# Cached attention on one core: K of a pack by two transfers instead of four, wide V by one instead of two

## The chip, the cores and the metric

The kernel runs on one core of a Trainium2 chip. The metric is the device time of one execution, in microseconds (us). A core has five engines that each work through a program of their own: PE (matrix products), ACT, DVE and POOL (elementwise work), and SP, which here does nothing but issue DMA transfers. Transfers run on 16 DMA engines, each of which takes packets from queues; one queue (q1) holds what SP issues, another (q10) what ACT issues. Engines wait for each other, and for transfers, by semaphores.

## The reference

Two independent attention blocks, A and B, of the same shape; their outputs stand side by side.

```python
B, Sq, D = 16, 64, 640            # batch, queries, model width
H, Sk, Dh = 32, 512, 128          # heads, cached keys, head width; all bfloat16
q = (x @ wq).reshape(B, Sq, H, Dh).transpose(0, 2, 1, 3)
scores = einsum("bhqd,bhkd->bhqk", q, k_cache) * Dh ** -0.5
o = einsum("bhqk,bhkd->bhqd", softmax(scores), v_cache)
out = o.transpose(0, 2, 1, 3).reshape(B, Sq, H * Dh) @ wo
# result: concatenate([out_A, out_B], axis=-1)
```

Each of the four caches (K and V of A and of B) has 16 × 32 × 512 × 128 values, 67.1 MB; every value is read once.

## The kernel before

**Tiling.** The work is cut into 128 packs. A pack is 4 heads of 2 batches (a batch pair), so 1 MB of K and 1 MB of V. Four packs with j = 0 to 3 cover 16 heads of one pair; eight pairs make a phase; four phases (two halves of the heads, two blocks) make the whole. The weights WQ and WO of the next phase are loaded while a phase ends.

**A pack's steps**, by the names in the code, with the lines of the profile: QP (L607, PE) projects the queries, KT (L621, DVE, two halves) transposes K in 32×32 blocks, S (L631, PE) forms the scores, EX (L650, ACT) takes the exponentials and row sums, RC (L663, DVE) and NM (L679, POOL) normalise, TR (L690, PE) and TE (L700, DVE) transpose the probabilities, PV (L714, PE) multiplies with V, OE (L722, ACT) copies out, OP (L734, PE) multiplies with WO and adds up.

**Loads.** LDK (L556) brings K of a pack into one of six buffers of `kn_ring`. It is four transfers of 256 KB: for each batch b and each half l, 32 rows of 8 KB go to the partitions 2b + l, 2b + l + 4, and so on. LDV (L567, L569) brings V into one of four buffers of `v_ring`, one transfer of 512 KB for each batch. Packs with j in `WIDE = (0, 1, 2)` have rows of 4 KB, one for each of 128 partitions (L567); the fourth has two rows of 2 KB in each partition (L569). LDX, LDWQ and LDWO bring x and the weights; some of these are issued by ACT.

**Order.** `build_plan` lists every operation with a due time in packs (`AT`) and sorts each engine's list by it; SP's list is sorted by the time from which a load may start. A V load may be issued once PV of the pack four before is done. K loads stand behind V loads in SP's list and have no wait of their own that lasts. From reads and writes the plan derives what each operation waits for. All transfers of a pack's K count on one semaphore, and so do those of its V. Because transfers of one semaphore may finish in any order, `wait_count` rounds a wait up to a whole pack by the table `PARTS`: four parts for K, two for V. KT therefore waits for all four K transfers, and PV for both V transfers:

```python
PARTS = dict(d_v=2, d_k=4)
...
def wait_count(d):
    part = PARTS.get(d.sem[0], 1)
    return -(-d.count // part) * part
```

A second program for very large or small sums stands behind the first and is not run here.

Of the kernel before, what the change touches and what calls it, by code (L numbers as in the profile page):

```python
# [14 lines left out]
SUM_MAX = 2.0 ** 40  # L15


PARTS = dict(d_v=2, d_k=4)


class Cfg:
    NK = 6
    NV = 4
# [36 lines left out]
def build_plan(dims, cfg, general):  # L60
# [12 lines left out]
    def add(eng, kind, idx, ts, reads=(), writes=()):  # L73
        op = Op(eng, kind, idx, ts, reads, writes)
        ops.append(op)
        at[(kind, idx)] = op
        return op

    def add_output(n):
        g, j = n // NJ, n % NJ  # L80
        final = n >= 0 and dims["FINAL"](g // NBP)
        for b in range(2):
            tv = n + AT["PV"]
            op = add("sp", "LDV", (n, b), tv - 0.3, [], [("v" if n >= 0 else "absent", n % cfg.NV, b)])
            loads.append((n - cfg.NV + AT["PV"] + 0.2 if n >= 0 else -99.0, 3, op))
        if n > -2:
            add("pe", "TR", n, n + AT["TR"], [("pn", i) for i in range(4)] + [("ident",)], [("B", 4), ("B", 5)])
        for b in range(2):
            add("dve", "TE", (n, b), n + AT["TE"][b], [], [("B", 4 + b), ("pT", b)])
        add("pe", "PV", n, n + AT["PV"], [("pT", 0), ("pT", 1), ("v", n % cfg.NV, 0), ("v", n % cfg.NV, 1)],  # L90
            [("B", 4), ("B", 5), ("B67",)])
        add("act", "OE", (n, 1), n + AT["OE"][0], [], [("B67",), ("oT", 1)])
        add("act", "OE", (n, 0), n + AT["OE"][1], [], [("B", 4), ("B", 5), ("oT", 0)])
        add("act", "ZO", n, n + AT["ZO"], [("zeros",)], [("B67",)])
        add("pe", "OP", n, n + AT["OP"], [("oT", 0), ("oT", 1), ("wo", j)], [("B67",)])
        if j == NJ - 1:
            bp = g % NBP
            add("dve", "OS", g, n + AT["OS"], [("acc", bp)], [("B67",), ("out_sb",) if final else ("acc", bp)])
            if final:
                add("act", "ST", g, n + AT["ST"], [("out_sb",)], [("out_dram", g)])  # L100
# [17 lines left out]
    for ph in range(NPH):  # L118
        twp = [ph * PH + j + (AT["WP1"] if ph else AT["WP0"]) for j in range(NJ)]
        for kt in range(dims["KT"] if ph else 0):  # L120
            ready = twp[-1] - PH + 0.5 if ph > 1 else NJ - 1 + AT["WP0"] + 0.5
            op = add("sp", "LDWQ", (ph, kt), twp[0] - 0.5, [], [("ws", kt, j) for j in range(NJ)])
# [17 lines left out]
    for n in range(-2, N):  # L140
        add_output(n)
        if n < 0:
            continue
        g, j = n // NJ, n % NJ
        add("pe", "QP", n, n + AT["QP"], [("xT", g % cfg.NX), ("wqp", j)], [("SB", 1)])
        add("act", "QE", n, n + AT["QE"], [], [("SB", 1), ("qs", n % cfg.NQ)])
        for i in range(4):
            op = add("sp", "LDK", (n, i), n + AT["KT"][0] - 0.9, [], [("kn", n % cfg.NK)])
            loads.append((n - cfg.NV + AT["PV"] + 0.2 - cfg.KLEAD, 2, op))
        for b in range(2):  # L150
            tk = n + AT["KT"][b]
            add("dve", "KT", (n, b), tk, [("kn", n % cfg.NK)], [("kt", n % cfg.NKT, b)])
        add("pe", "S", n, n + AT["S"], [("qs", n % cfg.NQ), ("kt", n % cfg.NKT, 0), ("kt", n % cfg.NKT, 1)],
            [("SB", i) for i in range(4)])
        for i in range(4):
            h = 4 * n + i
            te = n + AT["EX"][i]
            if general:
                add("dve", "MX", h, te - 0.002, [], [("SB", i), ("negmax", h % 4)])
            add("act", "EX", h, te, [("negmax", h % 4)] if general else [],  # L160
                [("SB", i), ("p", h % cfg.NP), ("rs", h)])
            add("pool" if n < N - 1 else "dve", "NM", h, n + (AT["NM"] if n < N - 1 else AT["NMZ"])[i], [("p", h % cfg.NP), ("recip", n % cfg.NR, i // 3)], [("pn", i)])
        for a in range(2):
            add("dve", "RC", (n, a), n + AT["RC"][a], [("rs", 4 * n + i) for i in ((0, 1, 2), (3,))[a]],
                [("recip", n % cfg.NR, a)])
# [158 lines left out]
class Clocks:  # L324
# [15 lines left out]
    def finish(self, eng, op):  # L340
        ck = self.clock[eng]
        self.val[op.sem] = self.val.get(op.sem, 0) + 1
        c2 = dict(ck)
        if op.dma:
            c2[op.sem] = op.count
        else:
            self.own[eng][op.sem] = op.count
            for s2, v2 in self.own[eng].items():
                if c2.get(s2, 0) < v2:
                    c2[s2] = v2  # L350
        part = PARTS.get(op.sem[0], 1)
        for k in range(op.count - 1, (op.count - 1) // part * part, -1):
            for s2, v2 in self.snap[(op.sem, k)].items():
                if c2.get(s2, 0) < v2:
                    c2[s2] = v2
        self.snap[(op.sem, op.count)] = c2


def wait_count(d):
    part = PARTS.get(d.sem[0], 1)  # L360
    return -(-d.count // part) * part


def order_waits(progs, need, base):
    ks = Clocks(base)

    def visit(eng, op):
        want = {}
        for d in need[id(op)]:
            want[d.sem] = max(want.get(d.sem, 0), wait_count(d))  # L370
        if any(ks.val.get(s, 0) < v for s, v in want.items()):
            return False
        ck = ks.clock[eng]
        cand = [(s_, v_) for s_, v_ in want.items() if ck.get(s_, 0) < v_]
        keep = list(cand)
        for w in list(cand):
            for o in keep:
                if o != w and ks.snap[o].get(w[0], 0) >= w[1]:
                    keep.remove(w)
                    break  # L380
        op.waits = keep
        ks.learn(eng, keep)
        ks.finish(eng, op)
        return True

    run_order(progs, visit)
# [46 lines left out]
def mha_kernel(nc, blocks, out, cfg=None):  # L433
    cfg = cfg or Cfg()
# [16 lines left out]
    for general in (False, True):  # L451
        dims = dict(NPH=NPH, NBP=NBP, NJ=NJ, KT=KT, FIRST=lambda ph: ph % NSUB == 0,
                    FINAL=lambda ph: ph % NSUB == NSUB - 1)
        plans.append(build_plan(dims, cfg, general))
    NK, NV, NKT, NX, NXN, NQ, NP, NR = (cfg.NK, cfg.NV, cfg.NKT, cfg.NX, cfg.NXN, cfg.NQ, cfg.NP, cfg.NR)

    with contextlib.ExitStack() as es:
        block = es.enter_context(nc.Block())

        def sb(name, shape, dt):  # L460
            return es.enter_context(nc.sbuf_tensor(name, shape, dt))
# [4 lines left out]
        kn_ring = sb("kn_ring", [128, NK, 2, 2048], BF16)  # L466
        kt_ring = sb("kt_ring", [128, NKT, 32, 2, 2, 16, 2], BF16)
        v_ring = sb("v_ring", [128, NV, 2, 16, DH], BF16)
# [31 lines left out]
        def pack_info(n):  # L500
            g, j = n // NJ, n % NJ
            ph = g // NBP
            return ph // NSUB, g % NBP, j, ph % NSUB * HPH + 4 * j
# [46 lines left out]
            return ins, ins  # L550

        def em_LDK(e, op):
            n, b, l = op.idx[0], op.idx[1] // 2, op.idx[1] % 2
            blk, bp, j, h = pack_info(n)
            src = blocks[blk][1][2 * bp + b, h:h + 4].rearrange("h (p l t) d -> l (h p) (t d)", l=2, t=32)[l]
            ins = e.dma_start(kn_ring[2 * b + l::4, n % NK].rearrange("p a c -> p (a c)"), src)  # L556
            return ins, ins

        def em_LDV(e, op):
            n, b = op.idx  # L560
            if n < 0:
                return None, None
            blk, bp, j, h = pack_info(n)
            src = blocks[blk][2][2 * bp + b, h:h + 4]
            dst = v_ring[:, n % NV, b]
            if j in WIDE:
                ins = e.dma_start(dst.rearrange("p t d -> p (t d)"), src.rearrange("h (p t) d -> (h p) (t d)", t=16))  # L567
            else:
                ins = e.dma_start(dst.rearrange("p (a t) d -> p a (t d)", a=2),  # L569
                                  src.rearrange("(a s) (p t) d -> (s p) a (t d)", s=2, t=8))  # L570
            return ins, ins
# [340 lines left out]
```

## Time and profile before

| what | value |
|---|---|
| runs, us | 747.2, 747.67, 748.57; median 747.67 |
| profiled execution, us from first to last instruction | 747.1 |
| busy: PE, DVE, ACT, POOL | 91%, 69%, 70%, 54% of the span |
| moved by DMA | 295.15 MB, mean 395 GB/s |
| queue of SP (q1) / of ACT (q10), share of 16 engines | 94.1% / 5.0% |
| granted TensorE clock | 0.985 |
| transfers of K / of V | 512 of 256 KB / 256 of 512 KB |
| V, issue to landing, median | 12.4 us (A), 13.3 us (B) |

The profile is of one execution; it gives no other time of that execution than its span, which is 0.57 us below the median of the timed runs. A busy share is an average over stages, so the prediction reads each stage by itself. "SPq" is SP's issuing of transfers; it lasts longer when the queue that it feeds is full. The packet records list every DMA packet with queue, start, duration and size, but not the engine that carried it.

### The profile page before, as it was taken

What the parts mean: (1) busy time and instruction counts of PE and PEld (TensorE: products, weight loads), DVE (VectorE), ACT (ScalarE), POOL (GpSimd) and SP (SyncE); (2) the same over time, 40 slices, a digit from 0 to 9 for tenths busy, and PEclk for the clock granted to TensorE, in tenths of its full rate; (3) what the DMA queues carried; (4) which work ended last, traced back from release to release, by engine and by line L of the source; (5) the groups of instructions that cost most, each with busy time, mean ns of one, the idle gap of its engine ahead of it and who ended that gap; (6) DMA issues with size and microseconds to landing.
All of it is one profiled execution on the core that took longest, in us unless ns stands there. A gap on an engine that the chain in (4) does not pass through costs nothing.

```text
span 747.1 us, 57746 instructions
## 1 busy us (share of the span) xinstructions
PE 681.3 (91%) x26518; PEld 530.5 (71%) x26518; DVE 514.9 (69%) x818; ACT 519.7 (70%) x1559; POOL 404.0 (54%) x580
## 2 busy tenths in 40 slices
PE   2779999999999999999988999999997999999994
PEld 2557777777777777777766777777775777777773
DVE  6437777777777677676755676677676677877773
ACT  1438787787777677766756777777775677777772
POOL 3635555655965545545674455455486555555550
PEclk9879999999999999999999999999999999999998
DMA  9999999999999999999999999999999999999970
GB/s 326 391 402 411 412 411 414 411 410 413 405 400 415 411 414 411 412 413 414 410 400 406 410 413 413 412 410 410 413 407 402 410 413 413 413 414 411 410 301 17
DMA packets 87518, 295.15 MB, mean 395 GB/s; under 512 B 13360, under 2 KB 28208, under 8 KB 71088
## 3 DMA queue, kind: packets, MB, share of 16 engines
q1 hardware_dynamic: 76064, 281.43, 94.1%
q10 hardware_dynamic: 11408, 13.27, 5.0%
q14 instruction: 37, 0.30, 0.1%
q8 instruction: 9, 0.15, 0.1%
HBM read 292.03 MB, written 2.62 MB: 394 GB/s over the span
## 4 chain that ended last, share of the span: by engine, by line
SPq 35%; PE 30%; DMA 19%; POOL 5%; issue 4%; ACT 3%; DVE 3%; ACTq 0%; DVEq 0%
SPq L556 23%; PE ps L714 8%; DMA kn_ring<-in_A_k_cache_dram 8%; PE ps L734 7%; PE ps L607 6%; SPq L567 6%; DMA v_ring<-in_B_v_cache_dram 5%; SPq L569 5%; PE ps L631 4%; DMA kn_ring<-in_B_k_cache_dram 4%; PE ps L690 4%; POOL pn_sb L679 4%; DMA ws_sb<-in_A_wq_dram 2%; ACT p_ring L650 2%; ACT oT_sb L722 1%
## 5 line engine op out<-in xcount | busy, mean ns | idle before, releaser
L679 POOL TENSOR_SCALAR pn_sb<-p_ring,recip 128x512 bf16<-128x512 bf16 x508 | 341.8, 692 | 305.5 <-DVE recip L663 305.4
L621 DVE STREAM_TRANSPOSE kt_ring<-kn_ring 128x1024 f32<-128x1024 f32 x256 | 313.5, 1230 | 146.1 <-DMA kn_ring<-in_B_k_cache_dram 103.9
L650 ACT ACTIVATE p_ring<-ps 128x512 bf16<-128x512 f32 x512 | 298.9, 598 | 28.7 <-DMA xn_ring<-in_B_x_dram 6.7
L700 DVE COPY pT_sb<-ps 128x1024 bf16<-128x1024 bf16 x258 | 163.6, 674 | 71.6 <-PE ps L690 68.5
L714 PE MATMUL ps<-pT_sb,v_ring 32*128 32x64 bf16 (+1 forms) x14528 | 163.8, 192 | 26.1 <-DMA v_ring<-in_B_v_cache_dram 11.7
L714 PEld LDWEIGHTS ps<-pT_sb,v_ring 32*128 32x128 bf16 (+1 forms) x14528 | 146.6, 92 | 43.0 <-DMA v_ring<-in_B_v_cache_dram 14.5
L607 PE MATMUL ps<-xT_ring,wqp_sb 128*128 128x128 bf16 x2560 | 166.6, 221 | 7.6 <-POOL xT_ring L596 7.3
L734 PE MATMUL ps<-wo_sb,oT_sb 128*128 128x320 bf16 x1040 | 166.6, 303 | 3.3 <-issue 2.3
L607 PEld LDWEIGHTS ps<-xT_ring,wqp_sb 128*128 128x128 bf16 x2560 | 158.0, 114 | 14.7 <-issue 7.5
L722 ACT ACTIVATE oT_sb<-ps 128x256 bf16<-128x256 f32 x260 | 85.6, 381 | 116.7 <-PE ps L714 116.7
L631 PE MATMUL ps<-kt_ring,qs_ring 32*64 32x512 bf16 x4096 | 139.5, 384 | 0.0
L690 PEld LDWEIGHTS ps<-ident,pn_sb 64*128 64x128 bf16 x4128 | 69.9, 95 | 76.4 <-ACT ps L726 38.4
L613 ACT ACTIVATE qs_ring<-ps 128x512 bf16<-128x512 f32 x128 | 76.5, 598 | 66.6 <-PE ps L607 66.4
L734 PEld LDWEIGHTS ps<-wo_sb,oT_sb 128*128 128x128 bf16 x1040 | 91.9, 98 | 40.9 <-issue 2.5
L650 ACT ACTIVATION_READ_ACCUMULATOR p_ring<-ps 128x1 f32 x512 | 106.0, 207 | 0.0
L690 PE MATMUL ps<-ident,pn_sb 64*128 64x64 bf16 x4128 | 83.8, 191 | 19.6 <-POOL pn_sb L679 9.1
L631 PEld LDWEIGHTS ps<-kt_ring,qs_ring 32*64 32x64 bf16 x4096 | 53.3, 104 | 29.2 <-issue 1.4
L726 ACT ACTIVATE ps<-zeros 128x256 f32<-128x256 bf16 x130 | 51.3, 394 | 0.0
L579 POOL COPY wqp_sb<-ws_sb 128x1280 bf16<-128x1280 bf16 x32 | 39.2, 1255 | 16.4 <-DMA ws_sb<-in_A_wq_dram 16.4
L663 DVE RECIPROCAL recip<-rowsum 128x3 f32<-128x3 f32 (+1 forms) x256 | 36.9, 144 | 3.9 <-ACT p_ring L650 0.6
L596 POOL COPY xT_ring<-xs_sb 128x640 bf16<-128x640 bf16 x32 | 22.9, 716 | 2.0 <-PE ps L607 2.0
L586 PE MATMUL ps<-ident,xn_ring 128*128 128x128 bf16 x165 | 14.9, 222 | 3.3 <-DMA xn_ring<-in_A_x_dram 3.3
(26 smaller groups left out, 65.7 us busy)
## 6 DMA issues: line engine op xcount, KB each, us to landing
kn_ring<-in_A_k_cache_dram SPq DMA_DIRECT2D x256, 256.0 KB
v_ring<-in_A_v_cache_dram SPq DMA_DIRECT2D x128, 512.0 KB, 12.4
kn_ring<-in_B_k_cache_dram SPq DMA_DIRECT2D x256, 256.0 KB
v_ring<-in_B_v_cache_dram SPq DMA_DIRECT2D x128, 512.0 KB, 13.3
ws_sb<-in_B_wq_dram SPq DMA_DIRECT2D x10, 512.0 KB, 16.3
wo_sb<-in_B_wo_dram ACTq DMA_DIRECT2D x8, 640.0 KB, 12.4
ws_sb<-in_A_wq_dram ACTq DMA_DIRECT2D x4, 640.0 KB, 17.4
wo_sb<-in_A_wo_dram SPq DMA_DIRECT2D x4, 640.0 KB, 14.1
```

The costliest lines, as they stand in the source:

```text
L556: ins = e.dma_start(kn_ring[2 * b + l::4, n % NK].rearrange("p a c -> p (a c)"), src)
L607: last = e.matmul(ps[:, 1, f * 128:(f + 1) * 128], w[:, kt, f, :], xT_ring[:, xs, kt, :], start=(kt == 0), stop=(kt == KT - 1))
L613: ins = e.activation(qs_ring[:, op.idx % NQ].rearrange("p f b q -> p (f b q)"), ps[:, 1, :], ACTF.Copy, scale=scale)
L621: ins = e.transpose(dst.rearrange("p c b (h l) -> p c h b l", h=8, l=2), src)
L631: last = e.matmul(ps[64 * b:64 * b + 64, i, :], qs_ring[rows, n % NQ, f, b, :], kt_ring[rows, n % NKT, :, f // 2, b, :, f % 2], start=(f = ...
L650: ins = e.activation(dst, src, ACTF.Exp, scale=1.0, accum_out=rowsum[:, h:h + 1])
L679: ins = e.tensor_scalar(dst, src, recip[:, h // 4 % NR, i:i + 1], 1.0, ALU.mult, ALU.mult)
L690: last = e.transpose(pt_bank(b)[:, 64 * c:64 * c + 64], pn_sb[rows, c, :], ident[rows, rows], tile_position=(64 * b, 0))
L700: ins = e.tensor_copy(pT_sb[:, b].rearrange("p t q -> p (t q)"), pt_bank(b))
L714: last = e.matmul(ps[:, 4 + i, 64 * b:64 * b + 64], v_ring[rows, n % NV, b, c, :], pT_sb[rows, b, c, :], start=(t == 0 and i < 2), stop=(t ...
L722: ins = e.activation(oT_sb[:, 2 * a:2 * a + 2, :], o_ps[:, 2 * a:2 * a + 2, :], ACTF.Copy)
L734: last = e.matmul(out_ps[:, s, :], oT_sb[:, i, :], wo_sb[:, 4 * j + i, s * NH0:(s + 1) * NH0], start=(j == 0 and i == 0), stop=(j == NJ - ...
```

## The change

K of a pack comes by two transfers, one for each half l, each with both batches: 64 rows of 8 KB into every second partition. V of a pack with 4 KB rows comes by one transfer of 1 MB for both batches. V of a pack with 2 KB rows stays at two transfers. The same bytes come from and go to the same places. Within a transfer, consecutive rows now come from the two batches by turns. The table `PARTS` becomes a function, since the number of V transfers now depends on the pack.

```diff
-PARTS = dict(d_v=2, d_k=4)
+def parts(sem):
+    if sem[0] == "d_v":
+        return 1 if sem[1] in Cfg.WIDE else 2
+    return 2 if sem[0] == "d_k" else 1
...
-        for b in range(2):
+        whole = j in cfg.WIDE
+        for b in range(1 if whole else 2):
             tv = n + AT["PV"]
-            op = add("sp", "LDV", (n, b), tv - 0.3, [], [("v" if n >= 0 else "absent", n % cfg.NV, b)])
+            op = add("sp", "LDV", (n, b), tv - 0.3, [],
+                     [("v" if n >= 0 else "absent", n % cfg.NV, i) for i in ((0, 1) if whole else (b,))])
...
-        for i in range(4):
+        for i in range(2):
             op = add("sp", "LDK", (n, i), n + AT["KT"][0] - 0.9, [], [("kn", n % cfg.NK)])
...
         def em_LDK(e, op):
-            n, b, l = op.idx[0], op.idx[1] // 2, op.idx[1] % 2
+            n, l = op.idx
             blk, bp, j, h = pack_info(n)
-            src = blocks[blk][1][2 * bp + b, h:h + 4].rearrange("h (p l t) d -> l (h p) (t d)", l=2, t=32)[l]
-            ins = e.dma_start(kn_ring[2 * b + l::4, n % NK].rearrange("p a c -> p (a c)"), src)
+            src = blocks[blk][1][2 * bp:2 * bp + 2, h:h + 4].rearrange("b h (p l t) d -> l (h p) b (t d)", l=2, t=32)[l]
+            ins = e.dma_start(kn_ring[l::2, n % NK].rearrange("p a c -> p (a c)"), src)
...
             if j in WIDE:
-                ins = e.dma_start(dst.rearrange("p t d -> p (t d)"), src.rearrange("h (p t) d -> (h p) (t d)", t=16))
+                src = blocks[blk][2][2 * bp:2 * bp + 2, h:h + 4]
+                ins = e.dma_start(v_ring[:, n % NV].rearrange("p b t d -> p b (t d)"),
+                                  src.rearrange("b h (p t) d -> (h p) b (t d)", t=16))
```

More of the change, by code (lines that the diff above doesn't have):

```diff
@@ L350, in finish @@
                     c2[s2] = v2
-        part = PARTS.get(op.sem[0], 1)
+        part = parts(op.sem)
         for k in range(op.count - 1, (op.count - 1) // part * part, -1):
@@ L359, in wait_count @@
 def wait_count(d):
-    part = PARTS.get(d.sem[0], 1)
+    part = parts(d.sem)
     return -(-d.count // part) * part
```

## The prediction

> **What bounds the kernel now.** I read the page's slices and queues first, then busy time by stage, then the waits, then SP's timeline, and last the packet records behind the page's part 3. The page:
>
> ```profile
> span 747.1 us, 57746 instructions
> ...
> PE   2779999999999999999988999999997999999994
> ...
> DMA  9999999999999999999999999999999999999970
> GB/s 326 391 402 411 412 411 414 411 410 413 405 400 415 411 414 411 412 413 414 410 400 406 410 413 413 412 410 410 413 407 402 410 413 413 413 414 411 410 301 17
> ...
> q1 hardware_dynamic: 76064, 281.43, 94.1%
> ```
>
> The 16 DMA engines are busy in every slice but the last two, at 400 to 415 GB/s, and PE is nearly as full. Which of the two sets the time is read by stage. The columns are the stretch, its length, busy time of each engine (instructions), the clock, the DMA share and GB/s:
>
> ```profile
> 60.00:195.00 135.00, 133.50 (x5383) 105.05 (x5376) 103.05 (x164) 106.76 (x319) 76.57 (x114) 1.00 1.02 411
> ...
> 235.00:365.00 130.00, 123.29 (x4775) 96.20 (x4768) 92.38 (x149) 93.58 (x286) 66.86 (x100) 1.00 1.03 413
> ...
> 590.00:722.00 132.00, 129.30 (x5172) 101.55 (x5170) 99.64 (x158) 99.52 (x301) 72.79 (x109) 1.00 1.02 412
> ```
>
> From 60 to 195 us PE is 98.9% busy: this is its floor. The scores (S, L631) of pack 5 start at 60.47 and those of pack 31 at 195.34 us: 134.87 / 26 × 4 = 20.7 us for four packs. From 235 to 365 it is 94.8% busy at the same DMA rate, so there DMA is the limit; from 590 to 722 it is 98.0%, both at once, and PE could give 132 × (98.9% − 98.0%) = 1.2 us. The waits say who waits for DMA:
>
> ```profile
> DVE kt_ring L621 <- DMA kn_ring<-in_B_k_cache_dram: 103.9, 64, 4.0
> ...
> DVE kt_ring L621 <- DMA kn_ring<-in_A_k_cache_dram: 42.0, 27, 2.8
> ...
> PEld ps L714 <- DMA v_ring<-in_B_v_cache_dram: 14.5, 15, 2.6
> ```
>
> 91 K transposes waited for K, 90 of them between 207 and 722 us. From pack 36 on (216 us), every pack's first transpose starts 0.02 us after the last update of its K semaphore. From pack 2 to 34 K lies ready 3 to 13 us early.
>
> Is DMA short of orders? SP's timeline (start, length, what, count):
>
> ```profile
> 606.20 1.06 SPq L567 DMA_DIRECT2D v_ring<-in_B_v_cache_dram  x2
> 607.30 2.40 SPq L556 DMA_DIRECT2D kn_ring<-in_B_k_cache_dram  x4
> ...
> 613.29 3.38 SPq L569 DMA_DIRECT2D v_ring<-in_B_v_cache_dram  x2
> 616.71 4.72 SPq L556 DMA_DIRECT2D kn_ring<-in_B_k_cache_dram  x4
> ```
>
> No. Four K issues take 2.4 us when nothing holds SP and up to 4.7 us here without any semaphore before them: SP stands at a full queue. The page's part 6 agrees, V lands a median 12.4 (A) and 13.3 us (B) after its issue, so some 10 us of work is always queued. The chain gives SP's issue 35% of the span, but that is back-pressure and not a cost of issuing. So the time is the DMA engines' packet time up to the last V landing at 731 us, and a tail of 16 us that the change doesn't touch.
>
> **What a packet costs.** The packet records of the SP queue (q1), in ns; the fourth column is mean × count per engine:
>
> ```
> bytes   packets  per engine  min  median  mean   us per engine
> 8192    16384    1024        307  313     315.2  322.8   (K)
> 4096    26496    1656        159  160     162.6  269.3   (wide V, WQ)
> 2048    16384    1024         84   86      87.2   89.3   (narrow V)
> 4       12832     802          9    9       9.2    7.4   (one per transfer and engine)
> ```
>
> 12,832 is 16 × 802, and SP issues 802 transfers (512 K, 256 V, 15 WQ, 4 WO, 15 X): each transfer ends in a 4-byte packet on each of 16 engines, the semaphore update. Its net price shows at the end, where one engine runs alone from 728.4 to 730.4 us: 2 KB packets follow each other by 80 ns, and after a 4-byte packet at 729.083 the next starts at 729.089, by 6 ns. A packet's last 3 to 4 ns overlap its successor, which is why busy shares exceed 1.
>
> **The change, part by part.** K: 512 transfers become 256. V: 96 wide packs of two become one each, 192 to 96. 352 transfers go. Rows, row lengths, bytes and destination bytes stay: 8 KB for K, 4 KB for wide V.
>
> 1. Update packets: 352 fewer on each engine × 6 ns = 2.1 us. The value is taken from the lone engine; by duration it is 352 × 9 = 3.2 us, and it is 0 if the updates hide beside other engines' packets. Of it 11 × 6 = 66 ns fall in each four packs (25 transfers become 14). PE's floor takes nothing of that while DMA is behind; between 60 and 195 us the gain only lengthens K's lead, which is spent after 195 us. From 590 us PE has 1.2 us to give, and about 8 groups × 66 ns = 0.5 us are asked.
>
> 2. Waits: none changes. KT waited for all four K parts before, and now for both; PV for both V parts, now for one. The second V issue had no wait of its own. Behind a V issue that waits for PV, SP still holds the same K, in the same order of packs. 0 us.
>
> 3. SP's time: the removed issues are 256 × 0.59 + 96 × 0.43 = 192 us of sequencer time (medians of L556 and L567), if the new ones cost the same; if a transfer of twice the rows costs twice, nothing is saved. Both lie behind the queued 10 us, so 0; without that cover a doubled issue would delay a landing by 0.6 us once.
>
> 4. Start: ACT's WQ loads (1 KB packets) share the engines with SP's K. SP now offers six 512 KB transfers in perhaps half the time, so WQ may come later; its first load has 40 packets per engine and took 6.7 us (1.21 to 7.91). With an 8 KB packet between every two it would take 40 × (0.306 + 0.044) = 14 us, 7 us more. PE would start later by that; the cover is the queue at 49.49 us, when SP had waited 4.3 us for PV and the load ahead of it landed at 56.68: 7.2 us queued. I take 0, at worst some 1 us.
>
> 5. Program fetch: the page's q14 packets carry 0.30 MB for about 3,760 counted instructions (DVE, ACT, POOL, SP), some 80 bytes each. 352 issues fewer are 28 KB, 3.4 packets of 8 KB × 0.309 = 1.0 us on whichever engine fetches. At 722 us the busy share drops to a third and one engine goes on to 730.4, so one straggler sets the landings; whether SP's fetch is on it I can't tell. 0, at most −1.0.
>
> 6. Order of rows: an engine's consecutive rows now alternate between two batches, whose rows lie 4 MiB apart (32 heads × 512 × 128 × 2 bytes); before it read 32 KB of V in one piece. No row of this trace alternates so far. The nearest is narrow V: two 2 KB rows 256 KB apart by turns, a mean 3.8% over its floor of 84 ns, against 2.3% for 4 KB and 2.0% for 8 KB. Per packet that is 3.2 ns, against 3.6 and 6.2: alternation does not show per packet. I take 0, as packets' extra time here goes by packets. The dear end is 3.8% for both: 8 KB to 320.7 (+5.5 × 1024 = 5.7 us), 4 KB to 165.0 (+2.4 × 1536 = 3.7 us), +9.4 us. The cheap end, by which two regions spread better and a third of the excess goes (a third of 6.2 × 1024 + 3.6 × 1536 = 11.9 us), is −4.0.
>
> The Trainium skill ("DMA: Bandwidth & Descriptors", Latency and other measured facts) speaks against this: copies whose rows lie 4 MiB apart ran at 103 GB/s and at 207 with 512 KiB. That rule is for all 128 rows at this pitch, and here only pairs are; no run here shows it yet.
>
> The same page (Rules for kernel authors) advises transfers of at least 1 MiB. Its fit of 2.0 us per transfer would promise 704 us for 352; the trace contradicts that, with 412 GB/s out of 256 and 512 KB pieces, since the fixed part is overlapped.
>
> **Sum.** Against the profiled span 747.1: −2.1 gives 745.0. The median of the runs is 0.57 above the span, and I leave that as it is: 745.6 us.
>
> **Rivals.** (a) Slower: alternating rows cost each K and wide-V packet time, in the DMA stage that bounds 207 to 731 us. It decides from 2.1 us / 2,560 packets = 0.8 ns per packet. At narrow V's rate it gives 747.67 + 9.4 − 2.1 = 755.0. For: the higher excess of narrow V per byte, and how little cancels the gain. Against: packets of the 16 engines are spread over 8 us of skew, so they don't march in step. At its worst every such packet takes twice as long, 1024 × 309 + 1536 × 159 ns = 561 us more, near 1,300 us; narrow V speaks against that, so 2%. The Trainium skill's rule on row pitch, above, in full would do this.
> (b) No change: updates are hidden, or packets grow by just under 1 ns: 747.6. The 6 ns between starts speak against the first.
> (c) Faster by more: the cheap end of step 6 or SP's fetch on the straggler: 747.67 − 2.1 − 4.0 = 741.6.
> (d) The change doesn't do what it says: a K source of 32 × 2 rows into 64 partitions runs on fewer than 16 engines. With eight, each would carry 8 more K packets a pack, 2.4 us × 128: 1,060 us. Both row counts divide by 16, so 1%.
>
> **How the numbers follow.** Forecast 48%, (c) 7%, (b) 17%, (a) 25% with its worst, (d) and a start beyond its cover 3%. A measurement here tells 0.2%, 1.5 us. Faster: 0.55; same: 0.17; slower: 0.28. The forecast's own range is 743.5 to 746.2 (updates at 9 ns and the fetch, to updates at 4 ns). The 8-in-10 range reaches up over most of (a), to 757, and down to 742.0, leaving out the tail of (c) and the worst of (a).
>
> **What would show it.** Right: 450 four-byte packets per engine instead of 802; 8 KB and 4 KB means still near 315 and 163 ns; the first K transpose still 0.02 us behind K from about pack 36; the last V landing near 729 us; the same 16 us of tail. Wrong: a mean above 316 ns for 8 KB packets or 164 for 4 KB; slices below 405 GB/s in the middle; V landing much sooner than 10 us after its issue, which would mean that SP fell short; or S of pack 4 starting over 7 us later than 55.55.

## The result, and the profile after

The changed kernel is slower: 751.33 us median (749.84 to 751.92, 4 runs) against 747.43 us (746.59 to 748.57, 4 runs) for the kernel before. The ratio is 1.0046, with a 95% interval of 1.0033 to 1.006. Run again beside the experiments it gave 1.0039 (1.0024 to 1.0053). The forecast was a gain of 2.1 us; what came is a loss of 3 to 4 us, inside the range and on the other side.

The page of the changed kernel, the lines that answer to those of before:

```profile
span 748.1 us, 57393 instructions
...
DMA  9999999999999999999999999999999999999980
GB/s 322 390 382 378 411 414 409 413 410 411 411 398 411 411 413 413 410 415 413 412 398 407 413 410 415 408 412 411 412 410 403 405 415 411 415 413 412 414 327 20
...
q1 hardware_dynamic: 70432, 281.41, 93.9%
q10 hardware_dynamic: 11408, 13.27, 5.1%
q14 instruction: 34, 0.28, 0.1%
```

The queue lost 5,632 packets, which is 16 × 352: all the update packets that the change meant to remove. The middle slices are as before. What differs is the third and fourth slice, 37 to 75 us: 382 and 378 GB/s, where before had 402 and 411.

The same stretches by engine (length, busy times, clock, DMA share, GB/s), changed kernel:

```profile
235.00:365.00 130.00, 124.70 (x4958) 97.95 (x4950) 94.35 (x150) 95.10 (x290) 68.55 (x102) 1.00 1.03 413
590.00:722.00 132.00, 129.56 (x5105) 101.65 (x5097) 100.35 (x158) 99.94 (x305) 71.25 (x106) 1.00 1.02 413
```

The DMA stages run at the rate of before, 413 GB/s. Now the start, first the kernel before:

```profile
52.00:54.00 2.00, 2.00 (x35) 1.66 (x28) 1.79 (x4) 1.87 (x8) 0.32 (x1) 1.00 1.01 406
54.00:58.00 4.00, 4.00 (x208) 3.00 (x206) 2.66 (x5) 2.78 (x9) 2.37 (x4) 1.00 1.01 407
58.00:60.00 2.00, 2.00 (x61) 1.85 (x61) 1.89 (x5) 1.64 (x6) 1.10 (x2) 1.00 1.06 430
```

and the changed kernel:

```profile
52.00:54.00 2.00, 1.07 (x84) 0.91 (x70) 0.00 (x0) 0.26 (x1) 0.41 (x1) 0.69 1.03 418
54.00:58.00 4.00, 2.63 (x94) 1.79 (x95) 0.24 (x1) 2.06 (x7) 0.00 (x0) 0.83 0.57 180
58.00:60.00 2.00, 2.00 (x11) 1.20 (x10) 2.00 (x4) 1.30 (x6) 0.77 (x2) 0.50 0.96 387
```

From 54 to 58 us the DMA engines are busy for 57% of the time and move 180 GB/s. For the rest of it they have nothing to do. By busy share that is 4 × (1.01 − 0.57) = 1.8 us. By the bytes of these lines it is 4 × (407 − 180) + 2 × (430 − 387) = 994 KB from 54 to 60 us, which take 2.4 us at 411 GB/s. Next to nothing gives them back: by the packet records the changed kernel is 0.16 MB behind the kernel before at 52 us, 1.12 MB at 60, 1.09 at 400 and 1.01 at 700. SP's timeline of the changed kernel says why they are idle:

```profile
43.91 0.59 SPq L547 DMA_DIRECT2D ws_sb<-in_A_wq_dram  x1
55.82 0.39 SPq L574 DMA_DIRECT2D v_ring<-in_A_v_cache_dram  x1
```

Between 44.5 and 55.82 us SP issues nothing. In its waits that is the longest one, 11.3 us, on PV, which frees the V buffer (total, times, longest):

```profile
SPq L574 <- PE ps L722: 107.2, 43, 11.3
```

Before, the same V was issued at 49.49 us after a wait of 4.3, the longest there. Its line, and the line of that wait:

```profile
49.49 0.81 SPq L567 DMA_DIRECT2D v_ring<-in_A_v_cache_dram  x2
```

```profile
SPq L567 <- PE ps L714: 42.5, 34, 4.3
```

PV is late because the whole of PE starts late: the scores of pack 0 start at 21.96 us and not at 14.91, those of pack 4 at 62.27 and not at 55.55. And PE is late because POOL, which arranges A's first WQ part for it, gets that part late. POOL before, and after:

```profile
7.96 2.45 POOL L579 COPY wqp_sb<-ws_sb 128x1280 bf16<-128x1280 bf16 x2 [6.40 <-DMA ws_sb<-in_A_wq_dram]
```

```profile
14.66 2.44 POOL L587 COPY wqp_sb<-ws_sb 128x1280 bf16<-128x1280 bf16 x2 [13.10 <-DMA ws_sb<-in_A_wq_dram]
```

The bracket gives POOL's idle time before the copy and what ended it: 13.1 us for WQ instead of 6.4.

Why WQ lands late shows in the packet records. WQ comes by ACT's queue in 1 KB packets, 40 per engine for the first part. In both profiles K's first packets go ahead of it. Before, the first WQ packets start in the half microsecond from 3.5 us, after the 256 KB transfers of that moment; after, with twice the rows in each, a microsecond later, from 4.5 us (ten of them earlier). Then WQ has most of each engine for a while. In the changed kernel this ends at 7 us: SP's queue is full from then on, and 8 KB packets take 85% of the engines' time, 1 KB packets 15%. In the kernel before it ends only near 8 us. By 7 us 717 WQ packets had started before and 528 after, on all engines together; the first part alone has 640. The engines are uneven. A 4-byte packet ends each engine's share of the part: before, all sixteen come between 5.5 and 7.5 us; after, eleven come by 8.3 us and the other five between 9.3 and 14.1. On those five the rest went by turns with 8 KB packets, and POOL has to wait for the last of them. The Trainium skill ("DMA: Bandwidth & Descriptors", Queues, rings and completion order) says that each engine goes round its queues packet by packet. The shares agree with equal turns: one packet of 309 and one of 46 ns by turns make 87% and 13%. (They would be the same with several of each at a turn.)

The profiled spans, 747.1 and 748.1, hide most of the loss, since the tail happened to be short this time. K of the last pack lands at 722.84 us before and at 725.44 after, 2.6 us later, but the ends differ by 1.0 only. PE's tail before:

```profile
735.00 2.32 PE L734 MATMUL ps<-wo_sb,oT_sb 128*128 128x320 bf16 x8
```

and after:

```profile
736.87 1.26 PE L742 MATMUL ps<-wo_sb,oT_sb 128*128 128x320 bf16 x8
```

The same eight matmuls took 2.32 and 1.26 us. Over the 12 profiles of this study the time from the last pack's scores to the end lies between 17.6 and 20.9 us. So single spans are not compared below; the landing of the last K, the rate of the landings and the timed ratios are.

### The profile page after: what moved, and what is told of

It reads as the page before. It is cut to its first block, busy times and chain, and to the rows that moved or that the text cites. A ratio compares the mean times of both kernels' runs of the same rounds, so it can differ in the third digit from the quotient of the medians.

```text
span 748.1 us, 57393 instructions
## 1 busy us (share of the span) xinstructions
PE 673.3 (90%) x26518; PEld 525.7 (70%) x26518; DVE 515.5 (69%) x818; ACT 519.9 (69%) x1559; POOL 404.0 (54%) x580
## 4 chain that ended last, share of the span: by engine, by line
PE 40%; DMA 28%; SPq 12%; POOL 8%; ACT 6%; DVE 3%; issue 3%; ACTq 0%; DVEq 0%
DMA kn_ring<-in_B_k_cache_dram 12%; PE ps L722 11%; PE ps L742 10%; PE ps L615 9%; POOL pn_sb L687 7%; SPq L562 7%; DMA v_ring<-in_B_v_cache_dram 5%; DMA v_ring<-in_A_v_cache_dram 5%; PE ps L698 5%; PE ps L639 5%; ACT p_ring L658 3%; DMA ws_sb<-in_A_wq_dram 3%; SPq L577 2%; DMA kn_ring<-in_A_k_cache_dram 2%; ACT oT_sb L730 2%
## 5 line engine op out<-in xcount | busy, mean ns | idle before, releaser
L722 PE MATMUL ps<-pT_sb,v_ring 32*128 32x64 bf16 (+1 forms) x14528 | 158.8, 192 | 23.9 <-DMA v_ring<-in_B_v_cache_dram 12.4
L722 PEld LDWEIGHTS ps<-pT_sb,v_ring 32*128 32x128 bf16 (+1 forms) x14528 | 143.3, 92 | 38.8 <-DMA v_ring<-in_B_v_cache_dram 15.5
L639 PE MATMUL ps<-kt_ring,qs_ring 32*64 32x512 bf16 x4096 | 137.3, 379 | 0.0
```

The source lines that it names most:

```text
L639: last = e.matmul(ps[64 * b:64 * b + 64, i, :], qs_ring[rows, n % NQ, f, b, :], kt_ring[rows, n % NKT, :, f // 2, b, :, f % 2], start=(f = ...
L722: last = e.matmul(ps[:, 4 + i, 64 * b:64 * b + 64], v_ring[rows, n % NV, b, c, :], pT_sb[rows, b, c, :], start=(t == 0 and i < 2), stop=(t ...
```

## The experiments

Two theories. The start theory: in the first 20 us the larger K transfers push WQ back, PE starts 7 us late, SP waits for PV, and the DMA engines run dry near 55 us; the rest of the run is even. The packet theory, later the steady theory: something costs a little in every pack. In each table row, "WQ" is the start of POOL's first copy, "scores" that of pack 0's, "share" the DMA share from 54 to 58 us, "K44–127" the time from the landing of pack 44's K to that of pack 127's (from pack 44 on, every pack of the changed kernel waits for its K), and "8 KB" the mean K packet from 250 to 715 us. Times are in us, the 8 KB packet in ns.

```
kernel             WQ     scores  share  last K   K44-127  8 KB    ratio to before (95%)
before              7.96  14.91   1.01   722.84   460.97   314.22  1
changed            14.66  21.96   0.57   725.44   461.20   314.90  1.0046 (1.0033 to 1.006)
changed_again      13.06  20.36   0.57   725.53   461.19   314.77  1.0039 (1.0024 to 1.0053)
k_two_only          8.11  16.03   1.01   722.77   461.26   315.19  1.0011 (1.0001 to 1.0022)
v_one_only          7.89  15.20   1.01   722.42   461.15   314.35  1.0002 (0.9992 to 1.0011)
start_by_four       8.07  15.38   1.02   723.02   461.38   315.17  1.0009 (1.0 to 1.0018)
start_by_two        7.66  15.34   1.02   722.67   461.09   314.41  1.0 (0.9989 to 1.0011)
start_as_changed   14.30  21.60   0.34   726.13   461.04   313.97  1.0052 (1.0039 to 1.0065)
wq_first            9.24  16.36   1.02   723.26   461.31   315.18  1.0004 (0.9992 to 1.0017)
k_two_one_batch    13.26  20.56   0.53   725.02   461.14   314.93  1.0035 (1.0022 to 1.0048)
v_by_four           6.70  14.26   1.02   722.60   461.25   314.22  1.0025 (1.0015 to 1.0035)
before_wq_first     7.37  14.67   1.03   722.52   461.11   314.52  1.0009 (0.9998 to 1.002)
```

**The parts of the change, one by one.** `k_two_only` has the change of K alone, `v_one_only` that of V alone. Where the number of transfers differs between packs, the plan keeps the first and last count of each pack in place of the fixed table. A function `k_parts(n)` gives the number of K transfers of pack n; the cuts below write its value out.

```diff
-        whole = j in cfg.WIDE      # k_two_only: V by two again
+        whole = False
...
-        for i in range(2):         # v_one_only: K by four again, em_LDK as before
+        for i in range(4):
```

> K of every pack by two transfers, V as before by two. Start theory: the first K transfers are handed over twice as fast, A's first WQ load lands near 14.6 us instead of 7.9, the scores of pack 0 start near 22 us instead of 14.9, the DMA engines run dry for about 2 us between 50 and 60 us, and the whole is 2 to 4 us slower than before. Packet theory (rows of two batches by turns make K packets 0.8 ns longer over the whole run): 1024 x 0.8 = 0.8 us lost against 256 x 6 ns = 1.5 us won, so 0.7 us faster than before.

Measured: 748.57 us against 747.95, ratio 1.0011. The start theory was wrong on this kernel: WQ came at 8.11 us. The packet records show that here WQ's packets, and not K's, were first at the engines (from 2 us on, K from 3 us).

> V of a 4 KB-row pack by one transfer, K as before by four. Start theory: WQ lands near 8 us and pack 0's scores start near 15 us as before, nothing runs dry, the time is within 1 us of before. Packet theory: 96 x 6 ns = 0.6 us won, 768 x 0.8 ns = 0.6 us lost, the same time as before; so both theories give no change, and if it is 2 us or more slower V's merging has a price that neither has.

Measured: 747.84 us, ratio 1.0002, no change, as both had it.

So neither part alone gives the loss, and who comes first at 2 us matters.

**The start put back, and the start alone.** `start_by_four` is the changed kernel with K of packs 0 to 3 by four transfers; `start_by_two` is the kernel before with K of packs 0 to 3 by two.

```diff
-        for i in range(2):
+        for i in range(4 if n < 4 else 2):     # start_by_four; start_by_two: 2 if n < 4 else 4
```

> The changed kernel, but K of packs 0 to 3 by four transfers as before. Start theory: WQ near 8 us, scores of pack 0 near 15 us, no dry stretch before 60 us, and the time falls back by 2 to 4 us to 746 to 748. Packet theory: 124 of 128 packs are as changed, so it stays at 751.

Measured: 748.56 us, half a us above the expected stretch, ratio 1.0009. Four packs of 128 bring back most of the loss. The packet theory falls with this.

> The kernel before, but K of packs 0 to 3 by two transfers, the only change. Start theory: pack 0's scores near 22 us, a dry stretch of about 2 us between 50 and 60 us, and 2 to 4 us slower than before. Packet theory: 124 of 128 packs are as before, so the time of before, 747.4.

Measured: 747.78 us, ratio 1.0. A miss for the start theory: WQ was first at the engines again, as in `k_two_only`, and nothing ran dry. Whether 512 KB transfers hurt depends on who is first.

**The changed kernel again, and its start with the rest of before.** `start_as_changed` has K by two for packs 0 to 3 and wide V by one, but K by four from pack 4 on.

> The changed kernel once more, beside the others of this call, for a second profile of its start and a closer ratio. Start theory, sharpened: whether A's first WQ load or the first K transfers get to the DMA engines first at 2 us decides when WQ lands; in this kernel K is ahead, WQ lands near 14.6 us, pack 0's scores start near 22 us, the engines run dry for some 2 us near 55 us, and the whole is 0.4 to 0.5% slower. Rival (steady theory): the start is as in the other variants (scores near 15 us) and the loss is spread over all packs, shown by K's landing from pack 44 to 127 taking 2 us or more longer than the 461.0 us of before.

Measured: 751.11 us median, 12 runs from 747.46 to 752.56; four of them lie below 749.5. WQ at 13.06 us, scores at 20.36, the share 0.57. Its packet records show K first at 2 us. Both profiles of this kernel have the late start; the spread of the runs fits two outcomes of the race, but only profiles tell them apart.

> K of packs 0 to 3 by two transfers and wide V by one throughout; K from pack 4 on by four as before. Its first 20 us are those of the changed kernel. Start theory: scores of pack 0 near 22 us, dry near 55 us, 2 to 3.5 us slower than before (749.5 to 751). Steady theory: K from pack 4 on and V alone cost nothing, so 747.9, as before.

Measured: 751.57 us (5 runs), ratio 1.0052, with the driest stretch of all:

```profile
54.00:58.00 4.00, 1.88 (x60) 0.85 (x60) 0.00 (x0) 0.94 (x3) 0.00 (x0) 0.82 0.34 125
58.00:60.00 2.00, 2.00 (x44) 1.33 (x37) 0.69 (x2) 1.58 (x5) 0.00 (x0) 0.50 0.97 297
```

This kernel has the transfers of `v_one_only` from pack 4 on, which cost nothing; only its first four packs differ, and it loses as much as the changed kernel. This settles where the loss is.

**WQ ahead by order.** In `wq_first` the changed kernel's SP issues K of pack 1 only after A's first WQ part has landed.

```diff
+    at[("LDK", (1, 0))].deps.append(at[("LDWQ", (0, 0))])
```

> The changed kernel, and SP issues K of pack 1 only when A's first WQ load has landed. Start theory: WQ lands near 6 us, pack 0's scores start at 12 to 15 us, nothing runs dry, and 2 to 3.5 us come back against the changed kernel: 747.5 to 748.8, as with packs 0 to 3 by four. Steady theory: 751 still.

Measured: 748.38 us, ratio 1.0004. WQ came at 9.24 us and the scores at 16.36, both later than expected, but early enough. One wait, and the loss is gone. SP's waits show it, and the longest for PV falls from 11.3 to 7.2 us; the engines don't run dry:

```profile
SPq L575 <- PE ps L723: 91.9, 38, 7.2
...
SPq L563 <- DMA ws_sb<-in_A_wq_dram: 6.9, 1, 6.9
```

```profile
54.00:58.00 4.00, 4.00 (x208) 3.18 (x207) 2.65 (x5) 2.16 (x7) 2.69 (x4) 1.00 1.02 409
```

**Where the forecast gain went.** `k_two_one_batch` takes the alternation away from K: 64 rows of one batch, 8 of its heads (the other batch's K is not read, so the scores are of other data).

```diff
-            src = blocks[blk][1][2 * bp:2 * bp + 2, h:h + 4].rearrange("b h (p l t) d -> l (h p) b (t d)", l=2, t=32)[l]
+            h = min(h, 24)
+            src = blocks[blk][1][2 * bp, h:h + 8].rearrange("h (p l t) d -> l (h p) (t d)", l=2, t=32)[l]
```

> K by two transfers of 64 rows, but all rows from one batch (8 of its heads; the other batch is not read, so scores are of other data), V as before: the transfers go from 512 to 256 with no rows of two batches by turns. If the alternation makes the 8 KB packets 0.8 ns longer, their mean from 250 to 715 us goes back from 315.2 to 314.3 ns and 1.5 us are won on k_two_only (747.0 against 748.6). If the engines as a whole are limited, so that update packets saved come back as longer data packets, the mean stays at 315.2 and the time at that of k_two_only.

Measured: the mean K packet is 314.93 ns, in the band of the kernels with K by two (314.77 to 315.19) and not of those with K by four (313.97 to 314.52). The alternation is not what lengthens the packets. The time, 1.0035 in 5 runs, is that of the late start: K was first at 2 us here, and WQ came at 13.26. So the late start needs neither V's merging nor two batches, only larger K transfers in front.

`v_by_four` goes the other way, with 192 transfers more than before.

```diff
+            b, c = (i // 2, i % 2) if n % NJ in WIDE else (i, 0)
...
+                ins = e.dma_start(v_ring[c::2, n % NV, b].rearrange("p t d -> p (t d)"),
+                                  src.rearrange("h (p t) d -> (h p) (t d)", t=16)[c::2])
```

> The kernel before, but V of a 4 KB-row pack by four transfers of 64 rows (even and odd partitions of each batch): 192 transfers more, so 192 more update packets on each engine, the other way from the change. If an update packet costs 6 ns among running engines as it does on a lone one, K's landings from pack 44 to 127 take 62 x 2 x 6 ns = 0.75 us more than the 461.0 to 461.15 us of the kernels with K by four, and the whole is 1.2 us slower. If the engines together are limited and the update only shortens the data packets beside it, that stretch stays within 0.2 us of 461.1, the mean 4 KB packet gets shorter than 162.5 ns by up to 0.75, and the time is that of before.

Measured: the stretch took 461.25 us and not 461.8, and the mean 4 KB packet fell from 162.53 to 161.94 ns, 0.59 ns × 1,536 = 0.9 us against the 192 × 6 ns = 1.15 us added. The packet records bear out the second reading. The time doesn't: 749.9 us, ratio 1.0025. The last K lands as early as ever (722.60), but its scores start 6.1 us later and not 4.7. SP issues back to back here, 2.5 us for four V and 2.5 us for four K in packs of 5.18 us:

```profile
606.34 2.51 SPq L586 DMA_DIRECT2D v_ring<-in_B_v_cache_dram  x4
608.89 2.69 SPq L571 DMA_DIRECT2D kn_ring<-in_B_k_cache_dram  x4
```

Yet SP's time is not shown to be what PE lost, for PE also takes longer where it waits for no transfer. From the scores of pack 5 to those of pack 31 it takes 136.77 us here and 134.87 before. What grew is PV. One pack before, and the same pack here:

```profile
95.82 1.21 PE L714 MATMUL ps<-pT_sb,v_ring 32*128 32x64 bf16 x128
```

```profile
95.93 1.42 PE L734 MATMUL ps<-pT_sb,v_ring 32*128 32x64 bf16 x128
```

Of the 19 wide packs between 60 and 195 us whose 128 PV matmuls are all on record, 12 have a pause of 0.1 to 0.2 us between two matmuls; before, 2 have. No wait in the profile goes with the pauses. What makes them is open.

**WQ first in the kernel before.**

> The kernel before, and SP issues K of pack 1 only when A's first WQ load has landed. Start theory: before has no dry stretch, so an earlier WQ has nothing to give, and the time is within 1 us of before. If instead an earlier start of PE were worth something by itself, it would be faster than before by over 1 us, and a version that beats both.

Measured: 748.24 us, ratio 1.0009. Nothing to give, as the start theory had it. No version here beats the kernel before.

## Why the prediction was wrong

**Step 4 (start) failed, and gave the sign.** The mechanism was named and its size was right: WQ 7 us later, PE 7 us later (7.05 for pack 0, 6.72 for pack 4). The size is partly luck: the text let an 8 KB packet go between every two of all 40 WQ packets, while here WQ stood behind K until 4.5 us, then had most of the engines, and went by turns only from 7 us on, on the engines that were not done. The cover was wrong. The prediction took 7.2 us of queued work at 49.49 us, from the landing of the load ahead, and set the loss at 0, at most 1 us. But that landing is the last engine's; the share begins to fall at 54 us, while the last queued load still landed at 57.48. And new work needs its own start: V issued at 55.82 fills the engines only from 58 us. V came 6.3 us later than before and the engines lost 2.4 us by bytes, so the cover was worth some 3.9 us (an estimate from these two) and not 7.2. K of pack 44 lands 2.4 us late and the last K 2.6 us. The text gave a start beyond its cover, together with (d), 3%.

**Step 1 (update packets) failed in size.** 352 packets per engine went, as forecast (450 left). Their 6 ns came from one engine that ran alone. Among 16 busy engines they are worth nothing that shows: with K by two, K44–127 took 461.14 to 461.38 us in six profiles, with K by four 460.97 to 461.25 in six. A gain of 83 packs × 2 × 6 ns = 1.0 us was due from K's transfers alone. The data packets beside them grew: the average of the 8 KB means is 315.02 ns in the first six and 314.28 in the other six, 0.74 × 1,024 = 0.8 us; and they shrank when updates were added to V. The reading that fits is that the engines together are limited at about 412 GB/s and one engine's saved nanoseconds go to its neighbours. It was shown by these two opposite changes, not by the limit itself. (A small slip beside it: from 590 to 722 us there are 132 / 20.7 = 6.4 groups of four packs and not 8, so 0.4 us were asked of PE there.)

**Step 6 and rival (a).** The direction of (a) came, but by another way. Packets of K did grow by just under the 0.8 ns that cancels the gain, but with rows of one batch too. So the forecast of 0 for alternation holds for K; for V it was not tried apart. The Trainium skill's rule on row pitch ("DMA: Bandwidth & Descriptors", Latency and other measured facts) shows nothing here: K's packets are no slower with rows 4 MiB apart by turns (314.77 to 315.19 ns) than without (314.93).

**Steps 2, 3 and 5.** No operation waits for more than before, but SP waits for PV longer: 48 us in all from 207 to 735 us, against 8 before. It has fewer issues to make and comes to the wait sooner. The engines moved 413 GB/s all the same, so the queue covered it. A transfer of twice the rows costs SP little more when nothing holds it: block A's K issues have a median of 0.60 us, against 0.59 before. Program fetch fell from 37 to 34 packets of q14, and nothing of it shows in the time.

Rival (b), hidden updates, describes the steady run, and `start_by_four` and `wq_first`, without the late start, come out at 1.0009 and 1.0004. Of the text's own signs of failure one came: the mean of all 8 KB packets of SP's queue, 315.2 ns before, is 316.3 and so over 316. Another, the scores of pack 4 over 7 us late, did not: at 6.72 us the loss was already there.

## What to carry to other kernels

A queue that covers a late start must be measured at the engine that runs dry first, less the time that new work takes to arrive, and not by when the last queued load lands. Where two queues share the DMA engines packet by packet, larger transfers of 8 KB rows in one can starve 1 KB rows in the other, so what PE needs first should be issued first, or the other queue should wait for it. A packet's price read from one engine at the end of a run is not its price while all engines are busy.

## What the runs showed of the hardware that was not expected

The order of the first packets of two queues at 2 us goes with 3 us at the end: of the profiles with K by two at the start and no wait for WQ, four have K first (WQ's copy at 13.06 to 14.66 us) and two have WQ first (7.66 and 8.11). What decides it is open. Sixteen engines that share one load need not end together: the first WQ part of the changed kernel ended on them between 6.6 and 14.1 us. Adding 6 update packets per engine to every four packs, or removing 8, left the rate of K's landings within 0.1%.
